# Chunked attention by units of 128 queries instead of 96: softmax turned on TensorE, values by chunk

## The chip, the cores and the metric

The kernel runs on one core of a Trainium2 chip. The metric is the device time of one execution in microseconds (us). A core has TensorE (PE, matmuls; its weight loads are shown apart as PEld), VectorE (DVE), ScalarE (ACT), GpSimd (POOL) and SyncE (SP, which issues the transfers here). TensorE reads SBUF and writes PSUM, which has eight banks of 512 floats in each of 128 partitions.

## The reference

Attention over 4 batches, 8 heads, 768 queries of 64 features, then a mixture of 4 experts on the 3072 x 512 result. Queries go in chunks of 32. A chunk sees its own 32 keys, 16 before and 8 after (fewer at the ends of the sequence), and 8 memory keys: 64 in all.

```python
for c in range(nc):
    ...
    k_full = np.concatenate([mem_k, k_ctx], axis=2)
    v_full = np.concatenate([mem_v, v_ctx], axis=2)
    scores = scale * np.matmul(q_c, k_full.transpose(0, 1, 3, 2))
    scores = scores - np.max(scores, axis=-1, keepdims=True)
    a = np.exp(scores)
    a = a / (np.sum(a, axis=-1, keepdims=True) + 1e-09)
    out[:, :, c_start:c_end] = np.matmul(a, v_full)
...
p = domain_probs / (domain_probs.sum(-1, keepdims=True) + 1e-09)
for e in range(E):
    h = np.maximum(x @ w1[e], 0.0)
    out += p[:, e:e + 1] * (h @ w2[e])
```

## The kernel before

**The experts** are nearly all of TensorE's work. Each operand is split into a high and a low part, and a product is three matmuls on the parts (high x high, high x low, low x high). From the second expert on, the products are formed from sums of operand blocks, seven in place of eight. In the profile these are the lines L817 (first products of the first block), L863 (second products by tokens), L883, L1123 and L1167.

**Attention** goes by units of 96 queries, three chunks: 8 units per batch, 32 in all. The first batch's 8 units are in the first block of the program; the other 24 are spread in windows among the experts of the batch before. A unit is done in these steps:

- Scores (`scores`, L485): 24 matmuls per unit, for 4 pairs of heads, 3 chunks and the 2 heads of a pair. Each has 64 rows and 32 weight columns, streams 64 keys and uses a part of TensorE's array of 64 rows by 32 columns, so six can stand side by side. The result has 96 partitions (queries) and 8 x 64 columns.
- Softmax: VectorE takes the maximum; ScalarE the exponential (in a window eight instructions, one per head, which also sum; in the first block one, with subtraction and sum on VectorE); VectorE or GpSimd multiply by the inverse sum.
- Band: each chunk's 64 probabilities are put where its keys lie in the 128 keys of the unit, and the rest of the band tile is zero. In the first block (`early_band`) ScalarE, VectorE or GpSimd write four pieces per unit; in a window only the third chunk goes through the band.
- Turn: probabilities must have keys on partitions. In the first block TensorE turns eight heads (`early_turn`, L1350, 128 band columns as weights, 96 columns streamed), and ScalarE or VectorE copy the result to `aT`. In a window VectorE turns seven 32-row blocks (L661).
- Values (`early_mix`, L1369; in a window `mixed`, L618): eight matmuls per unit, one per head, 128 keys against 64 value features, 96 columns streamed, two side by side in halves of the array.

A window (`window`) for unit u runs the scores of u and then the values of u-1 on TensorE. Each of the three batches has nine windows: the first without values, the last without scores.

**Order.** TensorE's order is written out: in the first block by the words of `FIRST_BLOCK` (W filler matmuls on zeros, S scores, T turn, X values, M and N first products on the units that are ready and on the rest, g and G second products), later by the order of calls. A planner places the other engines' and SP's operations around it by costs and due times, and draws some of them to DVE or POOL, ACT or DVE. SP issues transfers in the planned order. `AHEAD` says on how many units a product of the first block starts ahead of the others; such a product is in two parts.

**PSUM.** In the windows: three banks `moe_ps`, two `a_ps`, two `s_ps` for scores, one `x_ps` for values. In the first block the scores and the turns share two pairs of banks, `att_ps`.

## Time and profile before

| | |
|---|---|
| median of 3 runs | 1043.27 us (1041.76 to 1043.92) |
| the profiled execution | 1043.5 us, its span 1041.7 us |
| granted TensorE clock | 0.997 |
| TensorE busy | 1030.7 us, 99% |
| VectorE, ScalarE, GpSimd busy | 78%, 52%, 45% |
| transfers | 300.88 MB, mean 289 GB/s |

A row of the chain of waits gives start, length, the engine, what it writes, the line and the number of instructions. Records of TensorE's groups overlap each other, so lengths are read from the chain, where one piece follows another. The trace shows a matmul on plain 32-bit floats as two records, and so with its weight load.

### The profile page before, as it was taken

To read this page: it belongs to the slowest core of one execution; us is meant where nothing else is said; L and a number is where in the kernel's file an instruction comes from. 1 tells how busy PE (TensorE), PEld (TensorE's weight loads), DVE (VectorE), ACT (ScalarE), POOL (GpSimd) and SP (SyncE) were. 2 spreads that over 40 slices of the span, in tenths; PEclk is the share of its full clock that TensorE was granted. 3 is DMA by queue.
4 is the path that set the end of the run, shared out by engine and by line. 5 is a ranking of instruction groups with operands and counts; after the bars stand their busy time and mean duration, and the time that the engine had idled before them with its cause. 6 is when DMAs were issued, how large, how long until landed. Compare 5 with 4: busy or idle time off the path is not lost.

```text
span 1041.7 us, 21404 instructions
## 1 busy us (share of the span) xinstructions
PE 1030.7 (99%) x7899; PEld 988.8 (95%) x7899; DVE 809.4 (78%) x1358; ACT 539.3 (52%) x1426; POOL 464.9 (45%) x426
## 2 busy tenths in 40 slices
PE   7999999999999999999999999999999999999998
PEld 6988988989889999999999999999999999999998
DVE  6869786868976768678797968969699765949485
ACT  5636864746737656474755546445453534334241
POOL 2444654854605436172253606346072634626172
PEclk8999999999999999999999999999999999999999
DMA  9557989989979999999988878879679887879784
GB/s 297 179 206 238 376 335 359 357 333 352 347 279 384 357 306 333 326 342 328 309 259 303 282 259 278 279 246 296 232 241 305 287 262 247 280 237 275 250 253 144
DMA packets 185512, 300.88 MB, mean 289 GB/s; under 512 B 14816, under 2 KB 125504, under 8 KB 185408
## 3 DMA queue, kind: packets, MB, share of 16 engines
q1 hardware_dynamic: 185408, 299.51, 84.4%
q8 instruction: 63, 1.03, 0.4%
q14 instruction: 41, 0.34, 0.1%
HBM read 230.21 MB, written 69.26 MB: 287 GB/s over the span
## 4 chain that ended last, share of the span: by engine, by line
PE 93%; DVE 4%; DMA 1%; issue 1%; POOL 0%; ACT 0%; SPq 0%; DVEq 0%; POOLq 0%; ACTq 0%
PE a_ps L883 22%; PE moe_ps L883 16%; PE moe_ps L863 13%; PE a_ps L1167 12%; PE moe_ps L1167 10%; PE a_ps L1123 7%; PE moe_ps L1123 5%; PE moe_ps L817 3%; PE x_ps L618 2%; PE s_ps L485 2%; DVE A_lo L568 1%; DVE u L983 1%; DVE u L568 1%; DMA raw<-in_w_dram 1%; DMA qk_pair<-in_qk_dram 1%
## 5 line engine op out<-in xcount | busy, mean ns | idle before, releaser
L569 POOL TENSOR_TENSOR u<-u,routes 128x384 f32<-128x384 f32 x46 | 50.3, 1095 | 191.8 <-ACT u L552 191.5
L568 DVE TENSOR_TENSOR A_lo<-u,A_hi 128x384 fp32r<-128x384 f32 x139 | 118.2, 868 | 18.8 <-ACT A_hi L550 18.4
L863 PE MATMUL moe_ps<-w,h_hi 128*128 128x512 f32 x384 | 119.8, 393 | 0.0
L568 DVE TENSOR_TENSOR u<-moe_ps,u 128x384 f32<-128x384 f32 x120 | 66.2, 552 | 63.4 <-PE moe_ps L883 48.3
L569 POOL TENSOR_TENSOR raw<-raw 128x256 f32<-128x256 f32 x57 | 51.2, 899 | 127.1 <-DMA raw<-in_w_dram 83.1
L550 ACT COPY u<-a_ps 128x384 f32<-128x384 f32 x120 | 57.0, 475 | 78.8 <-PE a_ps L883 77.1
L550 ACT CAST A_hi<-u 128x384 fp32r<-128x384 f32 x144 | 73.3, 514 | 37.5 <-DVE u L983 31.1
L863 PEld LDWEIGHTS moe_ps<-w,h_hi 128*128 128x128 f32 x384 | 71.1, 188 | 14.8
L883 PE MATMUL a_ps<-xc_hi,ring 128*128 128x384 f32 x384 | 82.2, 336 | 0.0
L552 ACT ACTIVATE u<-u 128x384 f32<-128x384 f32 x96 | 50.2, 525 | 53.3 <-DVE u L568 52.7
L863 PE MATMUL moe_ps<-w,h_lo 128*128 128x512 f32 x192 | 75.0, 391 | 0.0
L569 POOL TENSOR_TENSOR us<-u,u 128x384 f32<-128x384 f32 x43 | 49.4, 1149 | 41.8 <-DVE u L983 20.3
L883 PEld LDWEIGHTS a_ps<-xc_hi,ring 128*128 128x128 f32 x384 | 67.8, 188 | 0.0
L1167 PE MATMUL a_ps<-A_hi,ring 128*128 128x384 f32 x256 | 65.8, 338 | 0.6 <-DVE u L983 0.6
L569 POOL TENSOR_TENSOR us<-u,us 128x384 f32<-128x384 f32 x43 | 49.5, 1151 | 30.2 <-DVE us L568 23.7
L569 POOL TENSOR_TENSOR u<-u,u 128x384 f32<-128x384 f32 x48 | 59.8, 1246 | 0.6
L569 POOL TENSOR_TENSOR u<-u,us 128x384 f32<-128x384 f32 x46 | 58.2, 1266 | 2.7 <-DVE A_lo L568 1.1
L639 ACT ACTIVATE s_sb<-s_ps,mx 96x64 f32<-96x64 f32 x192 | 57.1, 309 | 0.7
L568 DVE TENSOR_TENSOR acc<-a_ps,acc 128x384 f32<-128x384 f32 x52 | 28.8, 553 | 26.7 <-PE a_ps L1167 26.1
L883 PE MATMUL a_ps<-xc_lo,ring 128*128 128x384 f32 x192 | 48.9, 336 | 0.0
L1167 PEld LDWEIGHTS a_ps<-A_hi,ring 128*128 128x128 f32 x256 | 45.8, 188 | 2.4 <-DVE u L983 2.2
L569 POOL TENSOR_TENSOR w<-raw,w 128x512 fp32r<-128x512 f32 x25 | 35.9, 1443 | 26.7 <-ACT w L550 17.6
(237 smaller groups left out, 3110.8 us busy)
## 6 DMA issues: line engine op xcount, KB each, us to landing
ring<-k SPq DMA_DIRECT2D x144, 512.0 KB, 4.8
ring<-t SPq DMA_DIRECT2D x96, 512.0 KB, 6.0
ring<-w SPq DMA_DIRECT2D x72, 512.0 KB, 5.4
k<-w SPq DMA_DIRECT2D x48, 512.0 KB, 5.3
w<-w SPq DMA_DIRECT2D x32, 512.0 KB, 5.5
raw<-in_w_dram SPq DMA_DIRECT2D x62, 256.0 KB, 5.2
ring<-k SPq DMA_DIRECT2D x48, 256.0 KB, 4.1
qk_t<-in_qk_dram SPq DMA_DIRECT2D x24, 464.0 KB, 6.3
```

Of the source, the lines that this page charges most:

```text
L485: nc.tensor.matmul(s_ps.ap[c * CH:(c + 1) * CH, j * NPAIR + g, 0:KW], lhsT=x()[rows, g * UQ + c * CH:g * UQ + (c + 1) * CH], rhs=x()[rows, ...
L550: nc.scalar.copy(out(), x())
L552: nc.scalar.activation(out(), x(), func)
L568: ("DVE", t_dve(cols), lambda: nc.vector.tensor_tensor(out=out(), in0=x(), in1=y(), op=op)),
L569: ("POOL", t_pool(cols), lambda: nc.gpsimd.tensor_tensor(out=out(), in0=x(), in1=y(), op=op)),
L618: nc.tensor.matmul(x_out()[j * D:(j + 1) * D, g, :], lhsT=v_t.ap[:, h * D:(h + 1) * D], rhs=aT[:, j * NPAIR + g, :], start=True, stop=True,)
L639: now["plan"].add("ACT", t_act(KW) + 0.08, lambda h=h: nc.scalar.activation(s_sb.ap[:, h, :], s_in()[:, h, :], AF.Exp, bias=mx.ap[:, h, :] ...
L817: nc.tensor.matmul(ps.ap[:, lo:hi], lhsT=a[:, c * P:(c + 1) * P], rhs=x[:, c, lo:hi], start=(i == 0), stop=(i == len(steps) - 1),)
L863: nc.tensor.matmul(self.ps.ap, lhsT=h.ap[:, self.rows], rhs=w.ap[:, part, :], start=(i == 0 and k == 0), stop=(i == NF - 1 and k == 2),)
L883: nc.tensor.matmul(ps.ap[:, 0:SG], lhsT=a()[:, c * P:(c + 1) * P], rhs=y[:, k0 + c, :], start=(first and i == 0), stop=(i == len(steps) - ...
L1123: nc.tensor.matmul(ps.ap[:, cols], lhsT=x.ap[:, rows], rhs=w_ap[:, y, :], start=(begins and k == 0 and i == 0), stop=(k == NP2 - 1 and i = ...
L1167: nc.tensor.matmul(ps.ap[:, 0:SG], lhsT=w_ap[:, y, rows], rhs=x.ap, start=(begins and k == 0 and i == 0), stop=(k == NP2 - 1 and i == 2), ...
```

## The change

- **Units of 128 queries**, four chunks: 6 units per batch, 24 in all, six of them in the first block. A batch has 8 windows in place of nine.
- **Scores** (L470): 32 matmuls per unit of the same size as before, for eight parts of the array. The result fills 128 partitions. In a row of PSUM the 64 probabilities of the two heads g and g+4 stand so that both are 128 neighbouring columns after the softmax.
- **No band.** TensorE turns the two heads at once (`turned`, L491): four matmuls per unit with 128 probability columns as weights, 128 columns streamed. The result is one `moe_ps` bank, which ScalarE or VectorE copy to `aT`: on partitions 0 to 63 the keys of one head, on 64 to 127 those of the other. This is done in the windows too, so VectorE's turns go.
- **Values by chunk** (`mixed`, L506): 32 matmuls per unit, for 4 chunks, 4 features' places and the 2 heads. Each has 64 keys (rows), 64 value features (weight columns) and 32 streamed columns, in four 64 x 64 parts of the array. The values are laid out by chunk ahead of the launch, as a rearrangement of the input, with each chunk's own 64 keys.
- **Sizes of transfers:** q and k of a unit 640 KB (before 464), values 512 KB (before 256).
- **A window** runs on TensorE the values of u-2, then the turns of u-1, then the scores of u, and issues the values' transfer with the turns. The values share the banks `s_ps` with the scores (other columns); `x_ps` goes and `moe_ps` has four banks.
- **First block:** a new order and a new `AHEAD`; for units 1, 2 and 5 (`WIDE`) the exponential is in eight instructions as in a window; values share `att_ps` with scores. Filler matmuls: 67, before 98. `COMBINED_A` and `COMBINED_E` shift one block sum of the second weights.

How the change moves instructions is shown at three places. The first is TensorE's queue in a late window (`a_ps` and `moe_ps` with `ring` or `w` are experts' products). Before:

```order
L883 MATMUL a_ps<-xc_hi,w_1528 128x384 x4
L883 MATMUL a_ps<-xc_lo,w_1528 128x384 x2
L485 MATMUL s_ps<-qk_t 32x64 x24
L618 MATMUL x_ps<-aT_111,v_t 64x96 x8
L883 MATMUL a_ps<-xa_hi,w_1639 128x384 x4
L883 MATMUL a_ps<-xa_lo,w_1639 128x384 x2
```

And now:

```order
L865 MATMUL moe_ps<-w_1919,h_hi 128x512 x2
L865 MATMUL moe_ps<-w_1919,h_lo 128x512
L506 MATMUL s_ps<-aT_101,v_103 64x32 x32
L491 MATMUL moe_ps<-ident,s_sb 128x128 x4
L470 MATMUL s_ps<-qk_t 32x64 x32
L865 MATMUL moe_ps<-w_1662,h_hi 128x512 x2
L865 MATMUL moe_ps<-w_1662,h_lo 128x512
```

A window held 32 attention matmuls of two kinds, and now holds 68 of three, with the turns between values and scores.

The second is TensorE's queue in the first block, around the last values that the first half of the tokens needs (`xa`: that half's attention result). Before, ending with the values of the fourth unit and the scores behind it:

```order
L817 MATMUL moe_ps<-xa_hi,w_363 128x192 x8
L817 MATMUL moe_ps<-xa_lo,w_363 128x192 x4
L1369 MATMUL x_ps<-aT_113,v_t 64x96 x8
L817 MATMUL moe_ps<-xa_hi,w_372 128x192 x8
L817 MATMUL moe_ps<-xa_lo,w_372 128x192 x4
L1350 MATMUL att_ps<-ident,band_107 128x96 x8
L485 MATMUL att_ps<-qk_pair 32x64 x24
L1369 MATMUL x_ps<-aT_111,v_t 64x96 x8
```

And now, around the values of the third unit (third row from the end):

```order
L491 MATMUL moe_ps<-ident,spot 128x128 x4
L470 MATMUL att_ps<-qk_t 32x64 x32
L819 MATMUL moe_ps<-xa_hi,w_486 128x128 x8
L819 MATMUL moe_ps<-xa_lo,w_486 128x128 x4
L470 MATMUL att_ps<-qk_t 32x64 x32
L506 MATMUL att_ps<-aT_101,v_103 64x32 x32
L819 MATMUL moe_ps<-xa_hi,w_509 128x256 x8
L819 MATMUL moe_ps<-xa_lo,w_509 128x256 x4
```

The half is complete after three values groups, and the products ahead of that are on 128 tokens.

The third is SP's queue at the start (`w` and `in_w_dram`: weights; `pr`: routes). Before:

```order
L576 DMA qk_pair<-in_qk_dram 128x928 x4
L576 DMA v_t<-in_v_dram 128x512 x2
L576 DMA raw<-in_w_dram 128x512 x3
L576 DMA acc<-in_w_dram 128x512 x3
L576 DMA spot<-in_w_dram 128x512
L576 DMA pr<-in_probs_dram 128x24x4
```

And now, up to the third unit's value tile:

```order
L595 DMA qk_t<-in_qk_dram 128x1280 x2
L595 DMA v_103<-in_v_dram 128x1024
L595 DMA raw<-in_w_dram 128x512
L595 DMA qk_t<-in_qk_dram 128x1280
L595 DMA v_104<-in_v_dram 128x1024
L595 DMA raw<-in_w_dram 128x512 x2
...
L595 DMA qk_t<-in_qk_dram 128x1280
L595 DMA pr<-in_probs_dram 128x24x4
L595 DMA qk_t<-in_qk_dram 128x1280
L595 DMA v_103<-in_v_dram 128x1024
```

Fewer and larger transfers come first, and the first weights stand fourth.

The diff, cut to its core:

```diff
-UQ = 96
+UQ = 128
...
 FIRST_BLOCK = """
-W32 S0 S1 S2 W6 S3 W30 T0 W6 X0 T1 W12 X1 S4 W12 M1 T3 M5 X3 M2 T2 S5 X2 S6 M6 N7 N5 N4 N6 N0 N2 T5 N1 N3 S7 X5
-g0 T4 g1 G0 X4 T7 G1 X7 T6 g2 X6 G2
+W35 S0 S1 W18 T0 W6 X0 W5 T1 S2 M4 X1 M1 M2 W3 T2 S3 M6 S4 X2 M3 S5 N2 N0 N5 N7 N6 N3 T4 N4 T3 X4 N1 g0 X3 T5 g1 G0 g2 G1
+X5 G2
 """
-AHEAD = (0, 2, 2, 0, 0, 2, 2, 0)
+AHEAD = (0, 1, 1, 2, 1, 0, 1, 0)
...
+    def turned(t, s):
+        def fn():
+            for g in range(NPAIR):
+                nc.tensor.transpose(t.ap[:, g * UQ:(g + 1) * UQ], s.ap[:, g].rearrange("p j k -> p (j k)"), ident)
...
+    def mixed(x_ps, v_t, aT):
+        def fn():
+            for c in range(NCU):
+                for r in range(2):
+                    for m in range(2):
+                        for j in range(2):
+                            rows, g = slice(j * D, (j + 1) * D), 2 * r + m
+                            x0 = X_AT + r * UQ + c * CH
+                            nc.tensor.matmul(
+                                x_ps.ap[m * D:(m + 1) * D, j, x0:x0 + CH], lhsT=v_t.ap[rows, c, g, :],
+                                rhs=aT[rows, g, c * CH:(c + 1) * CH], start=True, stop=True,
+                            )
...
     def window(us, i, last=False):
-        band, aT = bands[0], aTs[0]
+        aT = aTs[0]
+        s_ps = new(lambda: late["s"], [P, 2, DM], "s_ps", 1, parts=2)
+        if i >= 2:
+            w = us[i - 2]
+            v_t = late_st[w]["v"]
+            pe(0.8, mixed(s_ps, v_t, aT), [v_t, "aT"], [(s_ps, 1)])
+        if 1 <= i <= len(us):
+            s_old, t_ps = late_st[us[i - 1]]["s"], bank()
+            pe(0.45, turned(t_ps, s_old), [s_old], [t_ps])
+            moved(lambda: aT.rearrange("p g q -> p (g q)"), lambda: t_ps.ap, DM, [t_ps], ["aT"])
+            want_v(us[i - 1])
         if i < len(us):
             u = us[i]
-            want_v(u)
-            s_ps = new(lambda: late["s"], [P, H, P], "s_ps", 1)
             qk_t = late_st[u]["qk"]
-            pe(1.0, scores(s_ps, lambda: qk_t.ap), [qk_t], [s_ps])
+            pe(0.55, scores(s_ps, lambda: qk_t.ap), [qk_t], [(s_ps, 0)])
...
-        for c in range(NCU):
-            rows = slice(c * CH, (c + 1) * CH)
-            for kb in ((0, 1), (1, 2), (1, 2, 3))[c]:
...
-                dve(lambda x=x, kb=kb, rows=rows: nc.vector.transpose(out=aT[kb * CH:(kb + 1) * CH, :, rows], in_=x()),
-                    268, [s_sb if c < 2 else ("band", 2)], [("aT", c)])
...
-    def early_band(u):
...
     def early_turn(u):
-        early_band(u)
...
+        s, t_ps = first[u], bank()
+        pe(0.45, turned(t_ps, s), [s], [t_ps])
+        moved(lambda: aTs[u % 2].rearrange("p g q -> p (g q)"), lambda: t_ps.ap, DM, [t_ps], [("aT", u % 2)])
```

(`pe(0.8, ...)` and the like are the planner's costs, which only order the other engines' work.)

## The prediction

> **What bounds the kernel now.** I read the page's busy times first, then the waits of TensorE, then the chain of waits.

> ```profile
> span 1041.7 us, 21404 instructions
> PE 1030.7 (99%) x7899; PEld 988.8 (95%) x7899; DVE 809.4 (78%) x1358; ACT 539.3 (52%) x1426; POOL 464.9 (45%) x426
> ```

> TensorE's waits (total, times, longest):

> ```profile
> PE att_ps L485 <- DMA qk_pair<-in_qk_dram: 1.8, 1, 1.8
> ...
> PE a_ps L1167 <- DVE u L983: 0.6, 2, 0.3
> ```

> These are the longest of all and the only one behind the first block: there nothing holds TensorE for a microsecond. So after about 30 us the time is the sum of what stands in TensorE's queue, and work taken from VectorE, ScalarE or GpSimd there is worth nothing. Before 30 us TensorE waits or runs filler, and there the chain to the first values counts.

> ```profile
> 0.00:30.08 30.08, 23.16 (x446) 20.72 (x447) 20.23 (x39) 17.63 (x36) 10.88 (x16) 0.89 0.83 274
> 110.00:300.00 190.00, 190.00 (x1346) 169.69 (x1345) 153.67 (x262) 114.03 (x314) 102.78 (x100) 1.00 0.93 346
> ```

> (Window, its length, busy time of PE, weight loads, DVE, ACT, POOL; then the clock, the DMA share, GB/s.) I therefore split the change into the late windows, where TensorE's own microseconds count, and the first block.

> **The late windows, before.** Rows of the chain (start, length, what):

> ```profile
> 206.38 1.04 PE a_ps L883 x6
> 207.43 1.04 PE moe_ps L883 x6
> 208.47 0.67 PE s_ps L485 x46
> 209.13 0.81 PE x_ps L618 x16
> 209.95 17.91 PE moe_ps L863 x78
> 227.85 0.67 PE s_ps L485 x46
> ...
> 253.69 0.81 PE x_ps L618 x16
> 254.50 1.24 PE a_ps L883 x6
> ```

> Scores take 0.67, values 0.81, and the first product behind them 1.24 where such a group otherwise takes 1.04: 0.20 for the change of array shape. A full window costs 1.68. Each of three batches has 7 full windows, one with scores alone (0.87) and one with values alone (1.01): 3 x 13.64 = 40.9 us.

> **The late windows, after.** A unit now has 32 score matmuls, 4 turns and 32 value matmuls; there are 6 units per batch instead of 8. What one matmul needs comes from the records of these tiles (ns: least, median, most; the profile has two records for each of these matmuls) and from the chain in the first block:

> ```profile
> L485 PEld LDWEIGHTS s_ps<-qk_t x1152: 102/106/107, 82.9 to 748.1; 64*32 64x32 f32 x192
> L485 PE MATMUL s_ps<-qk_t x1152: 216/216/241, 82.9 to 748.1; 64*32 64x64 f32 x192
> L618 PEld LDWEIGHTS x_ps<-aT,v_t x384: 132/137/137, 101.6 to 764.4; 128*64 128x64 f32 x192
> L618 PE MATMUL x_ps<-aT,v_t x384: 246/246/297, 101.6 to 764.5; 128*64 128x96 f32 x192
> ...
> 53.84 0.66 PE att_ps L1350 x8
> 54.50 5.50 PE moe_ps L863 x24
> 59.99 0.81 PE x_ps L1369 x16
> 60.80 0.81 PE att_ps L1350 x8
> ```

> *Turns.* Eight turns of 96 columns take 0.66, so 82.5 ns each, 0.86 ns per column; 128 columns are 110 ns. Four are 0.44, and I add 0.06 for the first weights: 0.50 us. Right behind values a turn group took 0.81, not 0.66: there the change of shape costs 0.15, so 0.59 in a full window.

> *Scores.* The 24 old matmuls went round 6 array tiles, 4 each. The 32 new ones go round 8 tiles, again 4 each. I keep 0.67. If eight tiles can't be fed in a round's time, the bound above is 0.67 x 32/24 = 0.89.

> *Values.* Before, 16 records over 2 tiles: 8 rounds, each as long as 96 columns need, 82.5 ns. Now 64 records over 4 tiles: 16 rounds, of 32 columns, 28 ns of stream. But each record also brings its own 64 columns of weights. The slowest old values record is 297 - 246 = 51 ns longer than the median, which is the first one waiting for its weights; for 32 weight columns the same difference is 241 - 216 = 25. So a 64-column load takes 51 ns or a little more (by the load records, 137 - 106 = 31 per 32 columns, 62). I take 57 for a round. The load was hidden behind 82 ns of stream; now the stream is hidden behind the load. The old 0.81 is 51 + 7 x 82.5 + 181 from the last round to the next group; the new is 51 + 15 x 57 + 127 (the last stream is 54 ns shorter) = 1.03 us. Bounds: 0.63 with rounds of 30 (stream alone), 1.41 with rounds of 82 (load and stream one after the other).

> A full window, in the order values, turns, scores, is then 1.03 + 0.59 + 0.67 + 0.20 = 2.49. A batch has four of these, one with scores alone (0.87), one with turns and scores (1.37), one with values and turns (1.62), one with values alone (1.23): 15.05, and 45.2 for three. **Late term: +4.3 us.** TensorE now also turns, and fewer units don't quite pay for it.

> What else moves there is covered. Seven VectorE turns per unit go, and the ScalarE copies into the band:

> ```profile
> L661 DVE STREAM_TRANSPOSE aT<-s_sb x96: 422/434/439, 92.5 to 757.8; 32x256 f32<-32x256 f32 x96
> qk_t<-in_qk_dram SPq DMA_DIRECT2D x24, 464.0 KB, 6.3
> v_t<-in_v_dram SPq DMA_DIRECT2D x32, 256.0 KB, 6.3
> q8 instruction: 63, 1.03, 0.4%
> ```

> That is 3 us of VectorE per unit, worth nothing while TensorE is full. The new waits: turns wait for a softmax multiplied one window earlier (208.47 to 227.85 is 19 us), values for a copy as old; all of TensorE's queue stands behind them, but neither is near. The value transfer now goes out with the turns, into a single place that the values just read have left; it needs 6.3 us of those 19. Transfers grow to 640 and 512 KB: 6 x 1152 - 8 x 720 = 1152 KB more per batch, 3.3 us at 346 GB/s. TensorE waits for no transfer there. Were that cover gone, it is 10 us over three batches.

> **The first block.** The chain before:

> ```profile
> 9.54 1.01 PE att_ps L485 x40
> 10.55 1.69 issue
> ...
> 12.68 3.31 PE x_ps L1270 x30
> 15.99 0.78 PE att_ps L1350 x8
> ...
> 19.78 7.96 DMA raw<-in_w_dram
> 27.74 0.02 issue
> 27.76 0.63 ACT w L550
> ...
> 28.99 1.04 POOL band L569
> ...
> 30.08 0.88 PE att_ps L1350 x8
> 30.96 0.67 PE att_ps L485 x46
> 31.63 1.16 PE x_ps L1369 x16
> ...
> 45.90 3.45 PE moe_ps L817 x24
> ...
> 72.58 10.40 PE moe_ps L817 x60
> ```

> TensorE is full only from 30.08, and what released it there was a band piece on GpSimd, itself behind a weight transfer. The values of 31.63 are the last that the first half of the tokens needs, and at 72.58 the second half's products start. So 40.95 us of work follow 31.63.

> After the change there is no band to lay, and three units make that half, not four. The third unit's value tile is the 17th transfer: ahead of it and with it stand five qk tiles (640 KB), three value tiles (512 KB), eight weights (256 KB) and the 48 KB of routes, 6832 KB or 7.0 MB. At the 274 GB/s of the first window it lands at 25.5, so I start these values at 26 instead of 31.63. Behind that start stand: products 14.5 us (three whole ones of 12 x 10.40/60 = 2.08; six parts at 1.37, what the x24 row leaves beside a whole one for 192 columns), values 4 x 1.23, turns 3 x 0.50, scores 0.87, the routes' turn 0.2, and 72 token matmuls at 5.50/24 = 0.23, 16.5: 38.5. The second half starts at 64.5: **first-block term -8.1 us.** Bounds: -11, if the transfers run as fast as 274/0.83 = 330 GB/s would have them (the same window's DMA share is 0.83) and land at 23; -2.4, if the values still start at 31.63 and only work is saved.

> **Instruction supply.** The rows "10.55 1.69 issue" (TensorE stopped 1.69 us inside a score group, with no wait) and "q8 instruction: 63, 1.03" (16.3 KB each) say that instructions come in blocks and can come late. A full window is now 2 x (64 + 4 + 64) = 264 records in 2.3 us, before 128 in 1.5. A block per 15798/63 = 251 records means that every full window crosses an edge; it only runs dry if the edge falls in the window's first records, by my estimate 1 of the 12 full windows at 1 us. Bounds 0 and 12 x 1.69 = 20. **+1 us.**
> [...]

> **Sum.** The profiled execution ran 1043.5 us (span 1041.7 and 1.8 around it), 0.2 over the median of 1043.27. +4.3 - 8.1 + 1 = -2.8: 1040.7 against that execution's own time, 1040.5 against the median, which I take. What a measurement can tell from no change is 0.2%, 2.1 us, so the forecast stands just outside.

> **Rivals.**
> *The startup doesn't shorten* (15%): transfers are larger, and the third values start no earlier than at 31.63; -2.4 + 4.3 + 1 = +2.9, 1046.2. For: the DMA share of 0.83 up to 30.08. Against: the old chain is held by the band and by filler, not only by transfers.
> *Rounds by the stream* (14%): the loads of four tiles overlap fully and don't set the round; 24 x (0.63 - 1.03) = -9.6, 1030.9. For: scores go round six tiles with 31 ns loads in little more than their stream. Against: the 51 ns of the first record.
> *Load behind stream* (9%): in a tile the next weights wait for the matmul; 24 x 0.38 = +9.1, 1049.6. Decides from a load longer than the stream, as here. Against: the large products load 95% of the time under a 99% busy TensorE.
> [...]
> [...]
> [...]
> *Instructions run dry* (6%): every full window stops as at 10.55; 20 in place of 1, 1059.5. Decides from more than a block per window, and 264 is just above it.

> **How the numbers follow.** The forecast has 52%, with its own range 1037 to 1044 (2 either way for the late term, 2.5 for the first block): 37 points of it faster by over 0.2%, 13 within, 2 slower. The startup rival: 10 slower, 5 within. Rounds by the stream: 14 faster. The three slow ones: 18 slower. One point is left over, faster. Together 0.52 faster, 0.18 within 0.2%, 0.30 slower. The range of 1031 to 1049 takes in the startup rival and about half of the two on the values' rounds, and leaves out the two far ones.

> **What would show it.** Values group of a full window at 1.0 to 1.1 us (0.63 or 1.41: a rival); turns 0.44 to 0.5 for four; scores 0.67; the second half's products starting at 63 to 66; no waits of TensorE over a microsecond after 35 us, none marked "issue" in the windows. Wrong: values far from 1.03, or a first half that starts after 28.

## The result: slower, and the profile after

The changed kernel takes 1053.35 us (median of 7 executions, 1050.04 to 1056.36) against 1043.71 for the kernel before (7 executions): a ratio of 1.0093, 95% interval 1.0071 to 1.0115, so slower by about 0.9% and clear of the noise. The forecast was 1040.5, with a range up to 1049. The profiled execution took 1056.36, its span is 1054.6 us. A second set of executions gave 1052.91 and a ratio of 1.0084 (1.0067 to 1.0102).

The head of the page of the changed kernel:

```profile
span 1054.6 us, 23060 instructions
PE 1042.7 (99%) x8936; PEld 1003.6 (95%) x8936; DVE 718.0 (68%) x1122; ACT 512.4 (49%) x1314; POOL 469.8 (45%) x427
PEclk8799999999999999999999999999999999999999
```

VectorE lost 91 us of work and ScalarE 27, and the time did not follow. The clock's row has a dip in its second slice (26 to 53 us) and a shallower one in its first. TensorE's waits (total, times, longest):

```profile
PE moe_ps L491 <- DVE s_sb L587: 2.2, 1, 2.2
PE att_ps L506 <- issue: 1.8, 2, 1.2
PE moe_ps L865 <- ACT w L569: 1.1, 1, 1.1
...
PE moe_ps L865 <- POOL w L588: 0.9, 1, 0.9
```

The chain has the full window of which the old form was shown at 208 us:

```profile
207.49 1.06 PE s_ps L506 x64
208.56 0.59 PE moe_ps L491 x4
209.14 0.79 PE s_ps L470 x53
209.93 17.93 PE moe_ps L865 x78
```

Values 1.06 (forecast 1.03), turns 0.59 (0.59), scores 0.79 (0.67). The chain in the first block, around the second and third unit's values:

```profile
14.71 1.49 PE moe_ps L819 x12
16.19 0.29 PE att_ps L506 x9
16.48 1.21 issue
17.69 1.01 PE att_ps L506 x55
18.71 4.09 PE moe_ps L819 x24
...
28.97 0.99 PE att_ps L506 x27
29.96 0.57 issue
30.52 1.28 PE att_ps L506 x37
```

The third values start at 28.97 where the forecast had 26, and TensorE stops inside the second and the third values with nothing that it waits for (issue). The 24 products of 18.71 take 4.09 us; on 128 tokens each, 12 of them took 1.49 at 14.71. The windows say why (length, busy time of PE, weight loads, DVE, ACT, POOL; then the clock, the DMA share, GB/s):

```profile
16.60:20.01 3.41, 2.32 (x67) 2.27 (x67) 3.06 (x6) 2.27 (x14) 1.34 (x1) 1.00 0.66 66
20.01:37.08 17.07, 16.50 (x307) 15.14 (x307) 8.24 (x15) 6.48 (x14) 2.68 (x3) 0.50 0.83 292
```

TensorE ran at half clock for 17.07 us, while it was 97% busy. Before the change it was at half clock for 6.8 us (9.3 to 16.1); there it stopped for 1.7 us and ran filler for 3.3.

**Where the time went.** I divided each profile into three sums. *Start* is when the second half's products (`xb`) begin. *Windows* is what attention adds behind that: from the last product record ahead of a group to the sixth behind it, less the products' own time. *Other* is all else by which product records follow each other later than their columns need. The products' own time is 921.4 us in every kernel here, and the three sums and it end at the last record's start.

| | start | windows | other |
|---|---|---|---|
| before | 72.4 | 41.1 | 3.0 |
| forecast of the change | 64.5 | 45.2 to 45.4 | 4 |
| changed | 71.3 | 47.8 | 10.3 |
| changed, a second profile ("again") | 70.9 | 48.5 | 6.3 |

So of 12.9 us between the two profiled executions, the windows took 6.7 (forecast 4.3), other 7.3 (1), and the first block gave back 1.1 (8.1). The first profile is of the longest of its executions (1056.36). With the second, of 1052.73, the three are 7.4, 3.3 and 1.5. In both the first block misses its forecast by the most, 6.6 to 7.0 us; the experiments go there first.

### The profile page after: what moved, and what is told of

Its sections match the earlier page's. It is cut to its first block, busy times and chain, and to the rows that moved or that the text cites. A ratio compares the mean times of both kernels' runs of the same rounds, so it can differ in the third digit from the quotient of the medians.

```text
span 1054.6 us, 23060 instructions
## 1 busy us (share of the span) xinstructions
PE 1042.7 (99%) x8936; PEld 1003.6 (95%) x8936; DVE 718.0 (68%) x1122; ACT 512.4 (49%) x1314; POOL 469.8 (45%) x427
## 3 DMA queue, kind: packets, MB, share of 16 engines
q8 instruction: 71, 1.16, 0.5%
## 4 chain that ended last, share of the span: by engine, by line
PE 95%; DMA 2%; DVE 1%; ACT 1%; issue 1%; POOL 0%; SPq 0%; DVEq 0%; POOLq 0%
PE a_ps L885 23%; PE moe_ps L885 17%; PE a_ps L1169 13%; PE moe_ps L865 12%; PE moe_ps L1169 10%; PE a_ps L1125 6%; PE moe_ps L1125 5%; PE moe_ps L819 4%; PE s_ps L506 2%; PE s_ps L470 1%; PE moe_ps L491 1%; DMA raw<-in_w_dram 1%; PE att_ps L506 1%; DMA t<-raw 1%; PE att_ps L470 0%
## 5 line engine op out<-in xcount | busy, mean ns | idle before, releaser
L587 DVE TENSOR_TENSOR A_lo<-u,A_hi 128x384 fp32r<-128x384 f32 x135 | 115.6, 871 | 19.5 <-ACT A_hi L569 19.2
L569 ACT COPY u<-a_ps 128x384 f32<-128x384 f32 x120 | 57.1, 476 | 116.2 <-PE a_ps L885 115.0
L588 POOL TENSOR_TENSOR raw<-raw 128x256 f32<-128x256 f32 x63 | 55.2, 877 | 107.3 <-DMA raw<-in_w_dram 89.1
L569 ACT CAST A_hi<-u 128x384 fp32r<-128x384 f32 x144 | 73.6, 514 | 30.3 <-DVE u L985 24.6
L588 POOL TENSOR_TENSOR us<-u,us 128x384 f32<-128x384 f32 x44 | 52.4, 1192 | 10.8 <-DVE us L587 8.0
L588 POOL TENSOR_TENSOR u<-u,u 128x384 f32<-128x384 f32 x46 | 56.8, 1238 | 0.5
L839 DVE SCALAR_TENSOR_TENSOR acc<-moe_ps,pr,acc 128x256 f32<-128x256 f32 (+1 forms) x50 | 28.3, 575 | 33.2 <-PE moe_ps L865 26.9
## 6 DMA issues: line engine op xcount, KB each, us to landing
raw<-in_w_dram SPq DMA_DIRECT2D x62, 256.0 KB, 6.0
```

What stands on the lines that cost most here:

```text
L569: nc.scalar.copy(out(), x())
L587: ("DVE", t_dve(cols), lambda: nc.vector.tensor_tensor(out=out(), in0=x(), in1=y(), op=op)),
L588: ("POOL", t_pool(cols), lambda: nc.gpsimd.tensor_tensor(out=out(), in0=x(), in1=y(), op=op)),
L839: dve(lambda: nc.vector.scalar_tensor_tensor(out=o.ap[:, cols], in0=ps_ap(), scalar=p_e, in1=o.ap[:, cols], op0=ALU.mult, op1=ALU.add), n_ ...
```

## Experiments on the first block

**again**: the changed kernel unchanged.

> The changed kernel once more. Theory A (what the two profiles suggest): the late windows cost TensorE about 6.7 us more than before in every execution (47.8 against 41.1); the first block is shorter by 6 to 8 us as long as the clock is granted in full, and gives most of that back in executions in which the clock stays at half for about five windows of 3.4 us behind 20 us. So an execution with a mean clock of 0.997 should take about 1050, one with 0.989 about 1055, and in this profile the second half's products should start near 71 if the clock is halved behind 20 us, and 64 to 67 if it is not. The wait of 2 us for weights near 274 us should be there again, since the order is the same. The tail's 384-column products, at 177 ns each in the first profile behind 846 us, should be at 177 again if the tail is slower by its code, and back at 173 if that was this one execution. Theory B (rival): the first block has not become shorter at all; then the second half's products start at 71 to 73 whatever the clock.

1052.91 us. The third values started at 30.40, the second half's products at 70.93, again with 17 us at half clock, now from 11.25:

```profile
11.25:28.32 17.07, 17.05 (x310) 15.81 (x310) 8.50 (x18) 9.56 (x33) 3.77 (x3) 0.50 0.91 288
```

Over the 13 executions of these two sets, those with a mean clock of 0.996 or more took 1050.0 to 1052.9, those with 0.990 or less 1053.1 to 1056.4, the two between 1052.7 and 1053.4. That goes with theory A; the start of the products alone fits both theories. The tail's products were back at 173 ns, so the 177 ns of the first profile (about 2 us) belong to that one execution. The wait for weights near 273 us was there again.

**fill**: 18 more filler matmuls ahead of the first turn.

```
-W35 S0 S1 W18 T0 W6 X0 ...
+W35 S0 S1 W36 T0 W6 X0 ...
```

> Eighteen more filler matmuls (2.0 us) ahead of the first turn, where TensorE waited 2.2 us for the softmax, so they should cost nothing there. Theory A: the half clock behind 20 us comes from a window of 3.4 us in which TensorE's array was used too little (idle, or at work on 64 x 32 and 64 x 64 parts only), and more full-array work ahead of it, or another place of the instruction edge, makes it rarer: with the clock full from 20 to 37 us the second half's products start at 64 to 67 in place of 71.3 and the time is 4 to 5 us under the slow executions of the changed kernel, 1048 to 1050. If the dip comes from the window of 16.6 to 20.0 alone, this filler changes nothing in it, and the clock still falls at 20. Theory B: the start is bound by transfers; products start at 71 with the clock full.

1054.99 us (1.0103, 1.0088 to 1.0118), half clock from 12.3 to 29.3, products at 71.0. The filler did not keep the clock up: here GpSimd did the softmax's last multiplication, and TensorE still waited 1.4 us. As the clock was not full, the start decides between neither theory.

**more_use**: filler raised to 110 matmuls.

```
-W35 S0 S1 W18 T0 W6 X0 W5 T1 S2 M4 X1 M1 M2 W3 T2 S3 M6 S4 X2
+W35 S0 S1 W44 T0 W8 X0 W6 T1 S2 M4 W4 X1 M1 M2 W6 T2 S3 M6 W4 S4 X2
```

> The changed kernel with filler in the first block raised from 67 to 110 matmuls: 26 more ahead of the first turn (2.9 us; TensorE waits there for 1.4 to 2.2 us), and 17 more on TensorE's path behind it (17 x 0.111 = 1.9 us): 2, 1, 4, 3, 4 ahead of later steps, and 3 that only fill a wait. Theory A, the clock: in the profiles so far the clock fell to half behind every 3.4 us stretch in which less than a third of the array's cycles were used (0.22 to 0.32 by rows x columns x streamed columns) and behind none with 0.34 or more, and came back only behind stretches with 0.56 or more; the first block's attention fills 0.35 to 0.4 without filler. So with more filler the clock stays full up to 30 us, or is at half for at most two stretches (7 us, against 10 to 17 in four profiles of the changed first block), the third unit's values start at 26 to 28.5 in place of 28.9 to 31.5, the second half's products at 66 to 69 in place of 71, and the time falls by 2 to 4 us to 1048.5 to 1051, though TensorE has 2 us more to do. Rival: the first block is bound by transfers or by its total work, and the clock follows; then the filler only adds, products start at 71 to 73 and the time is 1053 to 1055.

The miss is plain: 1054.76 us, 20.5 us at half clock, products at 75.0. The clock now stayed full up to 18.5 and fell behind a stretch in which TensorE stopped 1.6 us for instructions inside the scores of unit 2. The time is the rival's (1053 to 1055), and the start is later than either expectation had it.

**apart**: the third values between products, not behind scores.

```
-T2 S3 M6 S4 X2 M3 S5 N2 N0 N5
+T2 S3 M6 X2 M3 S4 N2 S5 N0 N5
```

> In the first block the scores of unit 4 no longer stand right ahead of the third unit's values: the order there is T2 S3 M6 X2 M3 S4 N2 S5 N0 in place of T2 S3 M6 S4 X2 M3 S5 N2 N0. In the profiles of the changed first block TensorE stopped inside these values (X2), marked issue, by 0.57, 1.83, 0.66, 1.64, 1.8, 2.9 and 2.4 us, with an instruction transfer landing 1.2 to 1.5 us ahead of each stop's end. Theory C, supply where it is dense: scores and values are 2 x 2 x 64 = 256 instructions in 1.9 us, as many as a block holds, and the next block can't come that fast; with a product between them the stop in X2 is under 0.5 us and no other of that size comes up ahead of 35 us, the second half's products start 1 to 2 us earlier (67 to 70), the time is 1050 to 1052. Rival: the stop falls where the edge of a block falls, whatever stands there; X2 stands 128 instructions earlier now, so the stop moves into the products or into the scores behind, of similar size, and the time stays at 1053. Against a gain in both: one change of array shape more, 0.1 to 0.2 us.

1049.46 us (1.0064, 1.0045 to 1.0082), 3.5 less than the changed kernel in its second set, and the best of the first-block edits; the two intervals overlap, so the gain is at the edge of what these runs can tell. The chain of this kernel:

```profile
19.31 6.63 DMA v<-in_v_dram
25.93 0.14 issue
26.07 1.39 PE att_ps L506 x64
27.46 2.86 PE moe_ps L819 x12
...
33.50 0.90 PE moe_ps L819 x4
34.40 0.36 issue
34.77 5.39 PE moe_ps L819 x29
```

The stop inside the third values is gone; one of 0.36 stands later, in products. The values start at 26.07, the forecast's 26, and what TensorE waits for there is their transfer, which lands at 25.93 (forecast 25.5). The clock was at half for 6.8 us in two pieces, and the products start at 67.7.

**wide_idle**: the filler by 25 instructions in place of 67.

```
-for _ in range(n):
-    nc.tensor.matmul(t.ap[:, 0:P], lhsT=idle, rhs=idle, start=True, stop=True)
+for k in [DM] * (n // 4) + [P] * (n % 4):
+    nc.tensor.matmul(t.ap[:, 0:k], lhsT=idle[:, 0:P], rhs=idle[:, 0:k], start=True, stop=True)
```

> The same filler time in the first block by fewer instructions: matmuls of 512 columns in place of four of 128, so 25 filler matmuls in place of 67, 84 instructions fewer (weight load and matmul each), a third of a block; all edges of blocks fall 84 instructions later in the work. If stops come where the edge falls (rival of the run before), the stop in X2 moves on by 84 instructions, out of X2's first half to its end or into the products behind (12 products have 24 instructions, so the stop there hides behind longer matmuls) and shrinks or goes; time 1050 to 1052. If they come where 256 instructions stand densely (theory C), the stop stays in X2 at 0.6 to 2.9 us and the time within 1 us of 1053.

1053.29 us (1.0091, 1.0072 to 1.0109). No stop for instructions is left in the first block, so stops come where a block's edge falls, though the time is that of theory C. Counting TensorE's records shows the edge directly: all 23 stops of 0.2 us and more in the first blocks of the 18 profiles stand 193 or 194 records over a multiple of 256, behind 449, 705, 1217 or 1473 records or one more. The clock was at half from 11.4 to 28.5 all the same, and the values started at 30.59. Behind that, at full clock and without a stop, stood 38.4 us of work up to 69.0: the forecast's 38.5 for that stretch was right.

**smooth**: apart and wide_idle together, and the filler ahead of the first turn and values raised to W36 and W8.

> Both changes to the first block that thin out instructions (the third values between products, filler in matmuls of 512 columns), and filler worth 36 + 8 matmuls of 128 ahead of the first two turns' work in place of 18 + 6, where TensorE waits (1.4 to 2.4 us ahead of the first turn). If the half clock behind 11 us comes from the stretch in which TensorE waits for the first softmax and nothing else keeps it down, the clock is now full from 4 to 30 us or falls for one stretch at most, no stop over 0.5 us is marked issue ahead of 35 us, the third unit's values start at 26 to 27.5, and the second half's products at 65.5 to 67, the forecast's 64.5 and 0.8 for one more change of shape; the time is 1047 to 1049. If the attention's small matmuls themselves keep the array's use too low, the clock falls behind 15 us all the same and the products start at 67.5 to 69.5, time 1049 to 1052.

1051.15 us (1.0071, 1.0055 to 1.0088). A stop of 2.3 us came up inside the second values, the clock was at half from 18.9 to 29.2, and the products start at 69.6. The second expectation nearly holds (67.5 to 69.5, 1049 to 1052), but the clock survived the first wait and fell behind the stop. The edge of a block moves with every edit ahead of it, so thinning at one place did not settle it.

**part_fill**: as wide_idle, but the filler uses a quarter of the array.

```
-    nc.tensor.matmul(t.ap[:, 0:k], lhsT=idle[:, 0:P], rhs=idle[:, 0:k], start=True, stop=True)
+    nc.tensor.matmul(t.ap[0:D, 0:k], lhsT=idle[0:D, 0:D], rhs=idle[0:D, 0:k], start=True, stop=True)
```

> As the kernel with filler in matmuls of 512 columns (wide_idle), but each filler matmul uses 64 rows and 64 columns of the array in place of 128 and 128: as many instructions and as much time, a quarter of the array. Theory U: the clock follows how much of the array is used in a stretch of 3.4 us (comes back from about 0.6, falls under a third). Then the filler at the start, which brought the clock to full at 4 to 6 us, no longer does (its share is 0.25 in place of 0.9), the clock stays at half until products fill a stretch, behind 25 us, the first scores and values run at half speed, and the second half's products start at 71 to 74 in place of 69.0; time 1054 to 1057. Rival B: the clock follows busy time whatever the part of the array; then it is full from 4 to 6 us up to about 11 as in that kernel, the products start at 68 to 70 and the time is 1053.

1057.49 us (1.0135, 1.0115 to 1.0155), products at 74.0: theory U, at or just over the upper end of its ranges. The first stretch of filler (columns as in the windows above), and the filler and the first three groups of values (duration in ns, least, median, most) in wide_idle:

```profile
1.30:4.70 3.40, 3.39 (x9) 1.23 (x10) 0.00 (x0) 0.71 (x1) 0.39 (x2) 1.00 0.81 289
...
L1272 PE MATMUL moe_ps<-idle x25: 219/379/634, 1.3 to 26.0; 128*128 128x512 bf16 x14, 128*128 128x128 bf16 x11
...
L506 PE MATMUL att_ps<-aT,v x192: 219/291/313, 11.5 to 31.5; 64*64 64x32 f32 x192
```

and in part_fill:

```profile
1.30:4.70 3.40, 3.39 (x8) 1.39 (x9) 0.00 (x0) 0.71 (x1) 0.39 (x2) 1.00 0.80 300
...
L1272 PE MATMUL moe_ps<-idle x25: 311/630/632, 1.3 to 27.2; 64*64 64x512 bf16 x14, 64*64 64x128 bf16 x11
...
L506 PE MATMUL att_ps<-aT,v x192: 291/291/313, 12.5 to 35.1; 64*64 64x32 f32 x192
```

Here no value matmul up to 35 us is a fast one (219). The filler of 512 columns starts every 427 ns throughout; in wide_idle it does so up to 4.6 us, and every 216 ns behind that. The clock reads 1.00 in these rows only because its records begin with the first change, at 38.5 us here and at 4.6 in wide_idle. From 1.3 to 4.7 us the engine was as busy in both (3.39 of 3.40 us); only the part of the array differs.

**lean_before**: the kernel before with 50 filler matmuls in place of 98.

```
-W32 S0 S1 S2 W6 S3 W30 T0 W6 X0 T1 W12 X1 S4 W12 M1
+W32 S0 S1 S2 W6 S3 W6 T0 W6 X0 T1 X1 S4 M1
```

> The kernel before with its filler matmuls cut from 98 to 50: 24 of those ahead of the first turn and both groups of 12 go (5.3 us of filler, all in places where TensorE would else wait). Theory A, the clock: it was the stretch of 12.7 to 16.1 us, full of filler, that brought the clock back before; without it the clock stays at half from about 9 or 13 us until products fill a stretch behind 25 us, 10 to 17 us in place of 6.8, the second half's products start at 74 to 77 in place of 72.4, and the time is 1045 to 1048. Rival: the clock at half costs nothing where TensorE waits for the softmax and the transfers anyway; then the products start at 71 to 73, and the time is 1043 to 1044.

1045.58 us (1.0023, 1.0011 to 1.0034). The half clock grew to 10.2 us as theory A has it, but the products started at 71.8, no later than before: there the rival is right, since the old first block waited for the band and the softmax. The old first block is not quite free of the clock, though: in the profile of draw_before (below) the clock never fell, and the products started at 70.8. The 0.2% came later, in other (6.3).

**What these say together.** From each trace the start of the second half's products can be added up: the start of the third values, the work behind them, half of the time that TensorE worked there at half clock (taking such work to last twice as long: in the trace of the changed kernel 128-column products start 213 ns apart from 20.0 to 37.1 us at half clock, and 109 to 112 ns apart at full clock), and the stops there. In the 12 profiles with the changed kernel's order, the work that this leaves is 38.0 to 38.9 us, the forecast's 38.5; in the three with the order of apart, which puts one more score group behind these values, it is 39.4 to 39.7. The third values start at 25.8 to 26.3 in four profiles (apart, both, sums_back, half_v), in which TensorE waits for their tile. In the other 11 TensorE comes to them later, at 28.9 to 34.7, though the tile lands at 23.5 to 26.2 wherever its landing is recorded.

For the changed kernel, the tile landed at 24.3 and the values started at 28.9, behind 8.9 us of work at half clock and a stop of 1.2. Behind that start come 38.0 of work, half of 7.6 us at half clock and a stop of 0.6: 28.9 + 38.0 + 3.8 + 0.6 = 71.3. Against the forecast's 26 + 38.5 this is 2.9 for the late start, 3.8 for the half clock, 0.6 for the stop, and 0.5 less work: the 6.8 that are missing. No run here kept the changed first block at full clock, so the forecast's 64.5 without half clock and stops is a sum and was not measured.

## Experiments on the late windows

**both**: values and scores in turn, a chunk of each at a time.

```
+for n in range(NCU):
+    mixed(s_ps, v_t, aT, (n,))(), scores(s_ps, lambda: qk_t.ap, (n,))()
```

> In the 12 windows that have both, the values of a unit and the scores of the next but one go to TensorE in turn, a chunk's 8 value matmuls and then 8 score matmuls, four times, and the turns follow behind. Before that: 1.07 for values, 0.59 for turns, 0.79 for scores, 0.20 for the next product's change, 2.65 a full window. Theory A (each array tile loads its next weights under its own stream, and values are paced by 64-column loads of 51 ns under 28 ns of stream, scores by 55 ns of stream over 29 ns of load): mixing hides the value loads under the scores' streams, 8 of the 16 value rounds of 58 ns shrink to about 30, and one start of a group (0.13) goes: a full window of 2.3 and the time 12 x 0.35 = 4 us less, about 1049. Rival 1: TensorE takes its instructions from a queue that drains here (scores slow down behind their 31st matmul record, with 8 to 17 ns a record in place of 7): 128 records without a long one between them then go at 10 to 14 ns each, 1.3 to 1.8 us for the two, and nothing to 0.5 is gained. Rival 2: mixing two tile shapes costs a change of shape each time (0.1 to 0.2, seven more of them), and the window gets longer, 2.9 to 3.5, the time 1056 to 1063.

1057.02 us (1.0118, 1.0098 to 1.0137). The chain of this kernel shows one quarter after the other:

```profile
226.54 0.36 PE s_ps L506 x16
226.90 0.27 PE s_ps L470 x16
227.18 0.36 PE s_ps L506 x16
...
229.09 0.59 PE moe_ps L491 x4
```

From 226.54 to the turns at 229.09 they take 2.55, where the two groups took 1.06 + 0.79 = 1.85: seven changes more of the tile's shape cost 0.70, 0.1 each. Rival 2 is right; nothing overlapped over a change.

**halves**: the scores in two halves, the turns between them.

```
+pe(0.3, scores(s_ps, lambda: qk_t.ap, (0, 1)), [qk_t], [(s_ps, 0)])
 pe(0.45, turned(t_ps, s_old), [s_old], [t_ps])
-pe(0.55, scores(s_ps, lambda: qk_t.ap), [qk_t], [(s_ps, 0)])
+pe(0.3, scores(s_ps, lambda: qk_t.ap, (2, 3)), [qk_t], [(s_ps, 0)])
```

> In a window the unit's scores come in two halves of 16 matmuls (32 records), one ahead of the turns and one behind them. Theory Q: scores slow down behind their 31st record (records 7 ns apart in rounds before, 8 to 17 ns behind) because TensorE has drained the instructions that were ready; the half behind the turns finds them ready again, so no half has records over 10 ns apart but for the rounds' edges, the two halves take 0.246 us of records each, and the slow part (0.31 for 32 records in place of 0.22) goes, 0.1 us a window; against it stands one change of array shape more, 0.1 to 0.15. So a full window of 2.6 to 2.75 and the time within 1 us of the changed kernel's 1053. Rival: the slow half belongs to the later heads (their PSUM columns or array tiles), and stays where g is 2 and 3; then the second half still has its records 8 to 17 ns apart, and a full window is 2.75 to 2.85.

1050.53 us (1.0057, 1.0037 to 1.0078). The chain:

```profile
227.83 1.06 PE s_ps L506 x64
228.89 0.39 PE s_ps L470 x32
229.28 0.59 PE moe_ps L491 x4
229.87 0.38 PE s_ps L470 x32
```

The times that theory Q forecast hold: both halves take 0.239 us from first to last record, in the second too no two records are over 10 ns apart but at a round's edge, and the slow part (64 records at once: 0.24 for the first 32, 0.40 for the others) is gone. The gain goes to the added change of shape: a full window is 2.64 in place of 2.65, the windows' sum 48.1. The 2 us of time, not clear of the spread, are thus not the windows'; other was 5.3 here.

**dve_turn**: the windows' turns back on VectorE.

```
-pe(0.45, turned(t_ps, s_old), [s_old], [t_ps])
-moved(lambda: aT.rearrange("p g q -> p (g q)"), lambda: t_ps.ap, DM, [t_ps], ["aT"])
+for n in range(4 * NCU):
+    q, k, x = slice(n // 4 * CH, (n // 4 + 1) * CH), n % 4 * CH, late_st[us[i - 1]]["s"]
+    dve(lambda q=q, k=k: nc.vector.transpose(...), 140, [x], ["aT"])
```

> In the windows the turn goes back to VectorE (16 instructions of 32 x 128 per unit), and TensorE's four turns and the copy behind them go; the first block is unchanged. Theory A: TensorE's queue sets the time of the late windows, so each of the 18 turns gives back its 0.59 us: full windows of 2.65 become 2.07, the windows' sum falls from 47.8 to about 37, and the time by about 10 us, to 1040 to 1045. VectorE gets 18 x 16 x 0.3 = 86 us more and is then about as busy as before the change (77%). Rival: VectorE's turns come late or delay the splits of the weights, and TensorE waits for them; then waits over a microsecond appear behind 80 us and the time falls by less than 5.

1047.96 us (1.0042, 1.0030 to 1.0054), 5.0 less. The windows fell to 40.0, by 7.8 (0.43 a turn, where 0.59 was expected). Other is 10.8, where the changed kernel's profiles have 10.3 and 6.3, so the time fell by half of what theory A has; a wait of 1.9 us for VectorE is there, as the rival has it. Rows of the page and of TensorE's waits:

```profile
PE 1028.7 (98%) x8864; PEld 989.7 (95%) x8864; DVE 795.2 (76%) x1426; ACT 502.8 (48%) x1296; POOL 448.6 (43%) x411
...
PE a_ps L1169 <- DVE u L985: 3.2, 4, 1.9
```

**apart_dve**: both gains together.

> The two edits that gained, together: turns back on VectorE in the windows (5.0 us less than the changed kernel by itself), and the third values between products in the first block (3.5 less by itself). If they add up, 1053 - 8.5 = 1044.5, within 1.5 us of the kernel before (1043.7), with windows at 36.4 us and the second half's products at 67.5 to 69. If VectorE's added work also stands in the first block's way or costs more waits behind it (they were 14.4 us with it, against 8 to 9), 1046 to 1048.

1053.53 us (1.0099, 1.0080 to 1.0117): they don't add up at all. The windows kept their gain (41.4), but the clock was at half for 17 us again (products at 70.3), and other is 15.2. Waits for VectorE behind the first block make up 9.1 of it; the longest:

```profile
PE a_ps L885 <- DVE w L587: 2.3, 1, 2.3
...
PE a_ps L1169 <- DVE u L985: 1.6, 5, 0.5
PE a_ps L1125 <- DVE Sb_lo L587: 1.4, 1, 1.4
PE a_ps L885 <- DVE u L587: 1.4, 2, 1.2
```

No version beat the kernel before.

## Experiments on the waits behind the first block

The first profile had a stall that the kernel before lacks. Its chain:

```profile
267.54 6.58 DMA raw<-in_w_dram
274.12 0.02 issue
274.14 0.63 ACT w L569
274.77 0.07 issue
274.83 1.28 POOL w L588
276.11 0.04 issue
276.16 1.22 PE moe_ps L865 x2
```

A weight came late, and the clock fell for a stretch behind the wait (276.01 to 279.43). With the waits of 2.0 us, that stretch at half clock (1.7) and the 177 ns products (2), 5.7 of the 10.3 in other are named.

**sums_back**: one block sum of the second weights back at its old place.

```
-COMBINED_A = (2, 2, 2, 1); COMBINED_E = {4: 1, 5: 2, 6: 2}
+COMBINED_A = (2, 2, 2, 2); COMBINED_E = {4: 1, 5: 1, 6: 2}
```

> Only the place of one block sum of the second weights goes back to where it was before (COMBINED_A and COMBINED_E as before). Theory A: the wait of TensorE for weights at 274 us (2.0 us, and the 3.4 us at half clock behind it, together about 3.7) comes from the order of the sums and transfers around 245 us; with the sum back no wait over 0.5 us stands between 265 and 285, and the time falls by 2 to 4 us, to 1047 to 1051. Rival: the wait comes from the larger q, k and value transfers or from the turns' copies, and then it stays and the time is that of the changed kernel within 1 us.

1051.37 us (1.0075, 1.0056 to 1.0093). The wait near 273 went, but one of 1.3 us for weights came up near 213: the gain is not clear of the spread.

**half_v**: half of each window unit's values are not transferred.

```
-dma(lambda: v_t.ap, lambda: v[u], ...)
+dma(lambda: v_t.ap[:, 0:NCU // 2], lambda: v[u][:, 0:NCU // 2], ...)
```

> In the windows only half of each unit's values are transferred (256 KB in place of 512; the values of the other two chunks are those of an older unit, so their results are another's). The order of everything is unchanged. 18 x 256 KB = 4.7 MB less, about what the change added. Theory A: the waits of TensorE for weights near 273 us (1.4 to 2.4 us in four profiles, none that long before 700 us in the kernel before) come from the larger attention transfers: then none over 0.5 us stands behind 200 us, and the time falls by 2 to 3 us to 1050 or 1051. Rival: they come from the order that the planner chose around 245 us (transfers behind splits that come late, with the DMA share at 0.50 from 240 to 250); then the wait stays, and the time is within 1 us of the changed kernel's 1053.

1052.54 us (1.0088, 1.0064 to 1.0111), and the wait stayed:

```profile
PE moe_ps L865 <- POOL w L588: 1.7, 1, 1.7
```

So it is not the larger transfers of values; those of q and k stayed larger here.

**draw_after** and **draw_before**: the planner's search behind the first block starts from another number.

```
-plan.run(ahead=LEAD) ... plan.run(last=True)
+plan.run(seed=2, ahead=LEAD) ... plan.run(seed=2, last=True)
```

> The changed kernel, but the planner's random search for everything behind the first block starts from another number. TensorE's order stays; the other engines' and the transfers' orders are drawn anew. Theory A: the waits of TensorE outside the windows (7.8 to 12.9 us behind the first block in five profiles, against 6.0 before) come from the order that the planner happened to draw, above all the wait for weights near 273 us; with another draw it is gone or elsewhere, and the time moves by 1 to 3 us either way, 1050 to 1056. Rival: the change itself causes them (larger transfers, turns' copies), and the wait near 273 stays and the time within 1 us of 1053.

> The same new start of the search for the kernel before. Theory A: its order was a lucky one or the best of several; another draw costs 1 to 3 us, 1044 to 1047, so that a part of the difference of 9 to 10 us belongs to the draw and not to the change. Rival: the draw moves nothing, 1042.5 to 1044.

The changed kernel takes 1052.10 us (1.0077, 1.0061 to 1.0092), and TensorE has no wait between 230 and 300 us, with all transfers as large as in the changed kernel: the wait came from the drawn order. Other is 6.9 there, so other waits took its place. The kernel before takes 1044.95 (1.0011, 1.0003 to 1.0020) and other is 4.9. In this one pair another draw moved each kernel by about 1 us, and the order of the kernel before is a good one (3.0, against 4.9 and 6.3 in its two variants; the changed kernel's variants with the turns on TensorE have 4.0 to 7.9).

## Why the prediction was wrong, step by step

- **What bounds the kernel, late**: right. Products cost 921.4 us in all kernels, and 91 us less on VectorE gained nothing. The other half of that step was too strong: VectorE's time was called worth nothing while TensorE is full, but giving VectorE 77 us in 288 short pieces brought waits for VectorE behind the first block of 4.3 us (dve_turn) and 9.1 (apart_dve), where the changed kernel has 0.8 and 1.1. Work that is free to take away was not free to add.
- **Late term, +4.3; measured +6.7 (+7.4 in the second profile)**: right in sign. Values were 1.06 for 1.03, with rounds 58 to 59 ns apart for the forecast's 57 (that the 64-column loads set the round was my estimate); turns 0.59 for 0.59. The mis-sized term is the scores, kept at 0.67 "if eight tiles can be fed"; they took 0.79, between that and the bound of 0.89, since their second half goes more slowly. That TensorE runs out of ready instructions behind 32 records is my reading of it and was not shown: halves shows that the slow part goes (0.239 for each half, 0.24 and 0.40 before) when the turns stand between. Eighteen score groups at 0.12 are 2.2 of the 2.4 missing.
- **First-block term, -8.1; measured -1.1 (-1.5 in the second profile)**: this step failed, even its weaker bound of -2.4. Its transfer and its work were sized right: the third value tile landed at 23.5 to 26.2 (forecast 25.5), and the work behind it is 38.0 to 38.9 (38.5). (The lower bound for the landing was 23, where 7.0 MB at 330 GB/s give 21.2.) What failed is the start at 26, which took TensorE to be free when the tile lands, and the full clock behind it. TensorE was at half clock for 17.1 us: the values started 2.9 late (at 28.97 in the chain, past the 28 that the prediction named as a sign of being wrong), and the work behind them took 3.8 longer. The row quoted for the first 30 us had a granted clock of 0.89, and I made no term of it, because the old first block waited at that time. The change took the waits and 31 filler matmuls out and packed small matmuls there: TensorE became the bound just where the clock was low.
- **Instruction supply, +1**: sized for what stands behind the first block, and there about right (0 to 1.5 us in a profile). It was not applied to the first block, where the row "10.55 1.69 issue" came from. Stops there sum to 0 to 3.6 us.
- **A late transfer term of nothing**: the larger transfers of values did cost nothing (half_v). But the planner's new order made a weight late, 2 us and a stretch of half clock in the first profile. That was no rival of mine, and could not be read from the profile of before.
- **Rivals.** "The startup doesn't shorten" is nearest in what happened, by a cause that it did not name, and its time (1046.2) is still 7 us short. "Load behind stream" has a nearer time (1049.6) by luck. "Rounds by the stream" (0.63) and "load behind stream" (1.41) are both refuted by 1.06. The third of the slow rivals, at 3%, took a fixed time for each record that no run shows: the 64 value records of 1.06 us are 16.6 ns each, with their starts 6 or 7 ns apart inside a round. "Instructions run dry" did not happen in every window: behind the first block a profile has two stops at most.

## What to carry to other kernels

Packing small matmuls into a start that used to wait turns waiting into TensorE work at whatever clock is granted there (half, for 17.1 us, in the changed kernel); read the clock of that stretch and price the work at it before counting a gain. Count matmuls by how much of the array they use: filler on a quarter of the array did not raise the clock here (its first recorded change came at 38.5 us in part_fill, at 4.6 with filler on the whole array in wide_idle). More filler alone did not keep it up either (17.0 us at half clock in fill, 20.5 in more_use). And where a planner sets the order, draw it again for both kernels before a difference of 1 or 2 us is put down to the change.
